# Attention read-out and gated FFN on one core: a new order for the loads of x, for the output of batch 0 and for the last rows

## The chip, the core and the metric

The kernel runs on one core of a Trainium2 chip. The metric is the device time in microseconds (us), the median of repeated runs; a lower time is better. A profile of one execution gives a trace, and every time "in the trace" below counts from the start of that execution's span, which is 228.7 us long.

## The reference, cut to what matters

There are two stages. The first is a cross attention between `x` (8 batches, 8 heads, 512 tokens, 64 channels) and `state` (the same with 32 slots):

```python
scores = scale * np.matmul(x, state.transpose(0, 1, 3, 2))
...                                  # softmax over the 32 slots
xread = np.matmul(a, state)          # 512 rows of each head
scores2 = scale * np.matmul(state, x.transpose(0, 1, 3, 2))
...                                  # softmax over the 512 tokens
sread = np.matmul(a2, x)             # 32 rows of each head
return np.concatenate([xread, sread], axis=2)
```

The second is a gated feed-forward block over the 8 x 544 rows, with the heads put side by side (512 channels, 1536 hidden):

```python
gate = 1.0 / (1.0 + np.exp(-(x @ w_gate)))
val = x @ w_val
return gate * val @ w_out
```

## The kernel before, in words

All instructions are written out in an order set by hand (`tc.manual_schedule()`); each engine runs its own in that order and waits on semaphores for the others. One batch at a time is in work.

**Loads.** `load_x(b, ...)` fetches the 1 MB of batch `b` into one of three `stg` buffers `xf`, with a DMA (L78) issued by the engine that is handed in. `cast_x` (L99) turns it to bf16 (`xb`, two buffers). The weight columns 0 to 255 of gate and value come by the SyncE queue in float32 (`wf`, L356) and are cast on an engine (L90). All other weights come by the GpSimd queue with the cast in the DMA: `load_w` (L83) and `load_wo` (L93). `gate()` (L87) is a one-column GpSimd copy that reads x of batch 1: what is behind it in the GpSimd queue starts when that has landed.

**Attention of batch b.** The transposed `xT` is made on TensorE for batches 0 and 1 (L114, L119), and from batch 2 on by four DMA transposes in the SyncE queue (`at_xT_dma`, L124). `S_mm` (L130) makes the scores in two halves, `S_exp` (L135) their exponentials on ScalarE, `n_sum` (L148, L150) and `n_mul` (L171) the normalised `ab` on VectorE. `aT_dma` (L192) transposes that by DMA; `at_Eb` (L141) is a cast on GpSimd. `n_tok`, `n_split` (L156 to L165), `sr_mm` (L208, L211), `sr_inv` and `sr_fin` (L216, L224) are the softmax over the tokens, whose result for all batches is kept in `XS`.

**FFN of batch b.** `xread` is never formed: the weights are multiplied with the state instead (`sw_mm`, L234), copied to `SW` (L272), and `gv_mm` (L286) multiplies `SW` with `aT`. `gv_th` (L296) is the tanh on ScalarE, `gv_glu` (L301) the product on VectorE. `out_mm` (L314) multiplies the result `glu` with `wo`: twelve calls a batch, call `k` doing four of the twelve hidden blocks of a chunk of 128 tokens; before, calls 0 to 2 make chunk 0, 3 to 5 chunk 1, and so on. The finished chunk is copied on ScalarE (L318) and stored through the SyncE queue (L320).

**Order.** A long hand-written prologue does the loads and the attention of batches 0 and 1 and their `gv_mm`. Then comes the loop over `b` from 1 to 8 with twelve steps `f`: step `f` of round `b` makes `gv_mm(b, f)`, `out_mm(b - 1, f)` and a part of the attention of batch `nb = b + 1`. Round 1 has no `gv_mm`. "Batch" 8 is the group of the 256 slot rows (`XS`), stored before in four pieces of 32 rows a chunk (L324). The last chunk of batch 7 is cut in three pieces (`out_last`, L327 to L340).

**Buffers.** The eight PSUM banks are shared out: two `gv`, one `outp` (OU), four `swp`, one `at`. `gv_mm` takes both `gv` banks, one for the gate, one for the value: the value bank is free again when `gv_glu` has read it. In round 1 the two `gv` banks hold the output of batch 0. `res`, the output copy in SBUF, has three buffers.

Of the kernel before, what the change touches and what calls it, by code (L numbers as in the profile page):

```python
# [8 lines left out]
FP = mybir.dt.float32  # L9
# [7 lines left out]
def kernel(  # L17
# [14 lines left out]
    nc = tc.nc  # L32
    B, H, S, D = x.shape
    Ns = state.shape[2]
    SC = S + Ns
# [7 lines left out]
    wp = ctx.enter_context(tc.tile_pool(name="wp", bufs=1))  # L43
# [26 lines left out]
    def load_x(b, eng, parts=1, hold=None):  # L70
        xf = stg.tile((128, H, 4, D), FP, name="xf")
        if hold is not None:

            hold.memset(xf[:, 0, 0, 0:1], 0.0)
        v = x[b].rearrange("h (p c) d -> p h c d", c=4)
        n = H // parts
        for i in range(parts):
            eng.dma_start(xf[:, n * i:n * i + n], v[:, n * i:n * i + n])  # L78
        xfs[b] = xf
# [2 lines left out]
        src = (moe_w_gate, moe_w_val)[w].rearrange("(k p) n -> p k n", p=128)  # L82
        nc.gpsimd.dma_start((wg, wv)[w][:, :, lo:lo + n], src[:, :, lo:lo + n])  # L83

    def gate():

        nc.gpsimd.tensor_copy(pre[:, 1:2], xfs[1][:, 0, 0, 0:1])  # L87

    def cast_w(w, cp):
        cp((wg, wv)[w][:, :, 0:256], wfs[w])  # L90
# [1 line left out]
    def load_wo(q):  # L92
        nc.gpsimd.dma_start(wo[:, 4 * q:4 * q + 4],  # L93
                            moe_w_out.rearrange("(k p) n -> p k n", p=128)[:, 4 * q:4 * q + 4])

    def cast_x(b, cp, lo, n):
        if b not in xbs:
            xbs[b] = xp.tile((128, 4, H, D), BF, name="xb")
        cp(xbs[b].rearrange("p c h d -> p h c d")[:, lo:lo + n], xfs[b][:, lo:lo + n])  # L99
# [21 lines left out]
    def at_xT_dma(b):  # L121
        xT = xT_tile(b)
        for c in range(4):
            nc.sync.dma_start_transpose(xT[:, :, c], xbs[b][:, c].rearrange("p h d -> p (h d)"))  # L124

    def S_mm(b, i, place):
        ps = held["S", b, i] = place[0].tile((128, 4, 2, 2, Ns), FP, name="Sp", tag=place[1])
        for jj in range(2):
            for c in range(4):
                nc.tensor.matmul(ps[:, c, :, jj], xTs[b][:, 2 * i + jj, c], sTz[:, b, 2 * i + jj], start=True, stop=True)  # L130

    def S_exp(b, i):
        if b not in E1s:
            E1s[b] = ap_.tile((128, 4, 2, 4, Ns), FP, name="E1")
        nc.scalar.activation(E1s[b][:, :, :, 2 * i:2 * i + 2].rearrange("p c e j n -> p (c e) j n"),  # L135
                             held["S", b, i].rearrange("p c e j n -> p (c e) j n"), AF.Exp, scale=scale)
# [9 lines left out]
    def n_sum(b, i):  # L146
        rs = ap_.tile((128, 8, 2), FP, name="rs")
        nc.vector.tensor_reduce(rs, halfE(b, i), AX.X, ALU.add)  # L148
        ri = held["ri", b, i] = ap_.tile((128, 8, 2), FP, name="ri")
        nc.vector.reciprocal(ri, rs)  # L150
# [16 lines left out]
    def n_mul(b, i, eng):  # L167
        if b not in abs_:
            abs_[b] = ap_.tile((128, 4, 2, 128), BF, name="ab")
        ri = held["ri", b, i]  # L170
        eng.tensor_tensor(abs_[b].rearrange("p c e (j n) -> p (c e) j n", n=Ns)[:, :, 2 * i:2 * i + 2], halfE(b, i),  # L171
                          ri.unsqueeze(3).to_broadcast((128, 8, 2, Ns)), ALU.mult)
# [125 lines left out]
    def gv_glu(b, f):  # L298
        if b not in glus:
            glus[b] = fp.tile((128, NF, n_of(b)), BF, name="glu", bufs=2, padded_shape=(128, NF, 512))  # L300
        nc.vector.scalar_tensor_tensor(glus[b][:, f], held["th", b, f], 1.0, held["gv", b, f][1], ALU.add, ALU.mult)  # L301
# [5 lines left out]

    def out_mm(b, k):
        c, f0 = k // 3, (k % 3) * 4
        if f0 == 0:  # L310
            place = SWP if b == B else GV if b == 0 else OU
            ops[b, c] = place[0].tile((128, 512), FP, name="outp", tag=place[1])
        for f in range(f0, f0 + 4):
            nc.tensor.matmul(ops[b, c], glus[b][:, f, c * 128:(c + 1) * 128], wo[:, f],  # L314
                             start=(f == 0), stop=(f == NF - 1))
        if f0 == 8:
            res = fp.tile((128, 512), FP, name="res")
            nc.scalar.activation(res, ops[b, c], AF.Copy, scale=0.5)  # L318
            if b < B:
                nc.sync.dma_start(rows_of(b, c), res)  # L320
            else:
                for i in range(4):
                    r0 = (4 * c + i) * SC + S
                    nc.sync.dma_start(out[r0:r0 + Ns], res[i * Ns:(i + 1) * Ns])  # L324

    def out_last(b, c):

        res = fp.tile((128, 512), FP, name="res")
        for lo, n in ((0, 256), (256, 128), (384, 128)):
            cs = slice(lo, lo + n)  # L330
            ps = p_sw.tile((128, 512), FP, name="outp", tag="swp")[:, :n]
            for f in range(NF):
                nc.tensor.matmul(ps, glus[b][:, f, c * 128:(c + 1) * 128], wo[:, f, cs],  # L333
                                 start=(f == 0), stop=(f == NF - 1))
            if lo == 256:
                nc.scalar.activation(res[:, cs], ps, AF.Copy, scale=0.5)
                nc.scalar.dma_start(rows_of(b, c)[:, cs], res[:, cs])
            else:
                nc.vector.tensor_scalar(res[:, cs], ps, 0.5, None, op0=ALU.mult)
                nc.sync.dma_start(rows_of(b, c)[:, cs], res[:, cs])  # L340
# [8 lines left out]
    sf = wp.tile((128, 16, D), FP, name="sf")  # L349
    nc.sync.dma_start(sf, state.rearrange("b h (u l) d -> (b h u) l d", l=16))  # L350
    load_x(0, nc.sync, 2)
    load_x(1, nc.sync)
    wfs = []
    for src in (moe_w_gate, moe_w_val):
        wf = wp.tile((128, 4, 256), FP, name="wf", bufs=2)
        nc.sync.dma_start(wf, src.rearrange("(k p) n -> p k n", p=128)[:, :, 0:256])  # L356
        wfs.append(wf)
    make_identity(nc, ident)
    nc.vector.memset(sTz, 0.0)
    for e in range(2):  # L360
# [24 lines left out]
    def pad(b, n=1):  # L385
        for e in range(2):
            rows = slice(e * 64, (e + 1) * 64)
            nc.gpsimd.tensor_copy(sTz[rows, b:b + n, :, e], sTc[rows, b:b + n])

    cast_x(0, vec, 2, 2)  # L390
    cast_x(0, pool, 4, 2)
    cast_x(0, act, 0, 2)
# [11 lines left out]
    S_mm(0, 0, SWP)  # L404
    S_exp(0, 0)
    warm(12, SWP)
    gate()
    load_w(0, 256, 256)
    S_mm(0, 1, AT)
    cast_x(1, act, 4, 4)  # L410
# [80 lines left out]
    load_wo(0)  # L491
    load_wo(1)
    load_wo(2)
    gv_glu(0, 5)
    sw_cp(1, 512, 1, 1, vec)
    sw_visit(1, 512, 512, 0)
# [2 lines left out]
    sr_mm(1, AT)  # L499
    sw_cp(1, 512, 1, 0, vec)  # L500
    gv_mm(1, 1, GV)
    load_x(3, nc.scalar)
    gv_th(1, 1)
    sw_visit(0, 1024, 512, 0)
    sw_visit(0, 1024, 512, 1)
# [59 lines left out]
    cast_x(3, pool, 0, 4)  # L565
    cast_x(3, pool, 4, 4)
    at_xT_dma(2)
    at_xT_dma(3)

    for b in range(1, B + 1):  # L570
        nb = b + 1 if b + 1 < B else None
        if b == 1:
            for i in range(2):
                S_mm(nb, i, (AT, GV)[i])
                S_exp(nb, i)
                n_sum(nb, i)
                n_mul(nb, i, nc.vector)
            aT_dma(nb)
        for f in range(NF):
            v, q = f // 6, f % 6  # L580
            if nb is not None and q == 0:
                sw_wide(nb, v)
                sw_cp(nb, v, 0, 0, act)
                sw_cp(nb, v, 0, 1, act)
            for first in (nb is not None and q == 0, nb is None or q > 0):
                if first and b > 1:
                    gv_mm(b, f, SWP if b == B and f % 2 else GV)
                    gv_th(b, f)
                    gv_glu(b, f)
                elif not first and (b < B or f < 9):  # L590
                    out_mm(b - 1, f)
            if nb is not None:
                if q == 0:
                    sw_cp(nb, v, 1, 0, vec)
                elif q in (1, 3, 4):
                    k = {1: 3, 3: 4, 4: 5}[q]
                    sw_cp(nb, v, k // 2, k % 2, act)
                if f in (1, 2) and b > 1:
                    S_mm(nb, f - 1, AT)
                    S_exp(nb, f - 1)  # L600
                elif f in (6, 7):
                    n_tok(nb, f - 6)
                    if f == 7:
                        n_split(nb, 0)
                elif f == 8:
                    n_split(nb, 1)
                elif f == 9:
                    sr_mm(nb, AT)
                    sr_inv(nb)
                elif f == 10:  # L610
                    sr_fin(nb)
                if f in (2, 4) and b > 1:
                    n_sum(nb, f // 2 - 1)
                elif f in (3, 5) and b > 1:
                    n_mul(nb, f // 2 - 1, nc.vector)
                if f == 3:
                    at_Eb(nb)
                    if nb + 2 < B:
                        load_x(nb + 2, nc.sync)
                elif f == 5 and b > 1:  # L620
                    aT_dma(nb)
                    if nb + 1 < B:
                        cast_x(nb + 1, pool, 0, 4)
                        cast_x(nb + 1, pool, 4, 4)
                        at_xT_dma(nb + 1)
# [33 lines left out]
```

The softmax here doesn't subtract the row's maximum and nothing guards it: scores larger than these inputs give would overflow.

## Time and profile before

The time is 231.14 us (median of 3 runs, 230.85 to 231.76).

| engine | busy, us | share of the span |
|---|---|---|
| TensorE (PE) | 218.5 | 96% |
| VectorE (DVE) | 141.4 | 62% |
| ScalarE (ACT) | 131.2 | 57% |
| GpSimd (POOL) | 42.5 | 19% |

The kernel moves 28.09 MB by DMA. Times to landing (from the issue to the last byte's semaphore), from the page's list of DMA issues: a load of x through SyncE 6.4 us in the median, the one through ScalarE (batch 3) 14.8, the one through GpSimd (batch 2) 9.4, the three pieces of `wo` 16.1 in the median.

How to read it: in a group line, the name left of the arrow is written and the one right of it is read, `xN` counts instructions, and the time in brackets is how long the engine stood idle before them and who ended that. SPq, ACTq and POOLq are the queues of instructions that issue DMAs. "PE busy" includes the pipeline, so a stop of TensorE is read from a bracket, not from the share.

### The profile page before, as it was taken

To read this page: it belongs to the slowest core of one execution; us is meant where nothing else is said; L and a number is where in the kernel's file an instruction comes from. 1 tells how busy PE (TensorE), PEld (TensorE's weight loads), DVE (VectorE), ACT (ScalarE), POOL (GpSimd) and SP (SyncE) were. 2 spreads that over 40 slices of the span, in tenths; PEclk is the share of its full clock that TensorE was granted. 3 is DMA by queue.
4 is the path that set the end of the run, shared out by engine and by line. 5 is a ranking of instruction groups with operands and counts; after the bars stand their busy time and mean duration, and the time that the engine had idled before them with its cause. 6 is when DMAs were issued, how large, how long until landed. Compare 5 with 4: busy or idle time off the path is not lost.

```text
span 228.7 us, 4759 instructions
## 1 busy us (share of the span) xinstructions
PE 218.5 (96%) x1856; PEld 113.0 (49%) x1856; DVE 141.4 (62%) x234; ACT 131.2 (57%) x246; POOL 42.5 (19%) x75
## 2 busy tenths in 40 slices
PE   7578999989999999999999999999999999999994
PEld 7463345444554444444444544454445444466743
DVE  2499889975368854886388647874687533422301
ACT  3587877655667476746666567556765444423311
POOL 1399921240015000600060006000200000000000
PEclk9889999999999999999999999999999999999999
DMA  6999999942866243724272431253122111121113
GB/s 218 347 177 174 215 281 246 186 74 59 211 224 221 49 92 123 247 46 95 93 231 82 83 118 46 73 88 116 46 72 69 47 46 49 50 80 55 49 33 105
DMA packets 38790, 28.09 MB, mean 123 GB/s; under 512 B 20976, under 2 KB 34160, under 8 KB 38768
## 3 DMA queue, kind: packets, MB, share of 16 engines
q1 hardware_dynamic: 32560, 21.44, 33.8%
q0 software_dynamic: 5024, 5.24, 13.0%
q10 hardware_dynamic: 1184, 1.11, 1.7%
q8 instruction: 14, 0.23, 0.4%
q14 instruction: 8, 0.07, 0.1%
HBM read 18.35 MB, written 8.91 MB: 119 GB/s over the span
## 4 chain that ended last, share of the span: by engine, by line
PE 78%; DMA 10%; POOL 6%; SPq 3%; issue 1%; ACT 0%; DVE 0%; POOLq 0%; ACTq 0%
PE outp L314 37%; PE gvp L286 28%; DMA xf<-in_x_dram 8%; PE gvp L289 5%; PE swp L234 4%; SPq L124 3%; DMA xT<-xb 2%; POOL Eb L141 1%; PE srp L211 1%; PE outp L333 1%; PE Sp L130 1%; POOL wg L83 1%; POOL ab L171 1%; POOL xb L99 1%; POOL wv L90 1%
## 5 line engine op out<-in xcount | busy, mean ns | idle before, releaser
L301 DVE SCALAR_TENSOR_TENSOR glu<-th,gvp 128x512 bf16<-128x512 f32 (+1 forms) x108 | 70.3, 657 | 63.9 <-ACT th L296 48.6
L314 PE MATMUL outp<-wo,glu 128*128 128x512 bf16 x396 | 97.8, 379 | 0.0
L296 ACT ACTIVATE th<-gvp 128x512 f32<-128x512 f32 (+1 forms) x108 | 61.6, 575 | 62.1 <-PE gvp L286 50.7
L286 PE MATMUL gvp<-aT,SW 128*128 128x512 bf16 x384 | 96.3, 380 | 0.1
L286 PEld LDWEIGHTS <-SW 128*128 128x128 bf16 x384 | 36.2, 98 | 45.1 <-issue 4.2
L314 PEld LDWEIGHTS <-glu 128*128 128x128 bf16 x396 | 37.5, 98 | 41.0 <-issue 0.4
L272 ACT CAST SW<-swp 128x512 bf16<-128x512 f32 (+1 forms) x78 | 42.2, 579 | 2.9 <-PE swp L234 1.6
L318 ACT ACTIVATE res<-outp 128x512 f32<-128x512 f32 x33 | 19.7, 597 | 19.7 <-PE outp L314 17.5
L141 POOL CAST Eb<-E 128x256 bf16<-128x256 f32 x32 | 12.4, 429 | 98.7 <-ACT E L135 98.7
L99 POOL CAST xb<-xf 128x1024 bf16<-128x1024 f32 (+1 forms) x13 | 14.6, 1147 | 20.6 <-DMA xf<-in_x_dram 20.6
L272 DVE CAST SW<-swp 128x512 bf16<-128x512 f32 x20 | 13.4, 683 | 2.7 <-PE swp L234 2.7
L171 DVE TENSOR_TENSOR ab<-E,ri 128x512 bf16<-128x512 f32 x14 | 13.7, 980 | 0.1
L156 DVE TENSOR_REDUCE E<-E 128x128 f32<-128x512 f32 x12 | 12.3, 1033 | 0.0
L234 PE MATMUL swp<-wg,sTc 64*32 64x256 bf16 (+1 forms) x256 | 11.9, 328 | 0.2 <-ACT E L135 0.2
L148 DVE TENSOR_REDUCE rs<-E 128x16 f32<-128x512 f32 x16 | 10.8, 678 | 0.9 <-ACT E L135 0.9
L234 PEld LDWEIGHTS <-sTc 64*32 64x32 bf16 x512 | 6.2, 91 | 10.4 <-issue 7.7
L135 ACT ACTIVATE E<-Sp 128x512 f32<-128x512 f32 x16 | 9.6, 608 | 1.8 <-PE Sp L130 1.8
L234 PE MATMUL swp<-wv,sTc 64*32 64x256 bf16 (+1 forms) x256 | 10.4, 324 | 0.2 <-POOL wv L90 0.2
L130 PE MATMUL Sp<-sTz,xT 128*128 128x64 bf16 x128 | 7.0, 199 | 1.7 <-ACT xT L119 0.7
L130 PEld LDWEIGHTS <-xT 128*128 128x128 bf16 x128 | 6.1, 102 | 4.9 <-ACT xT L119 0.8
L216 DVE RECIPROCAL r<-srp 128x128 f32<-128x128 f32 x8 | 7.6, 951 | 1.1 <-PE srp L211 1.1
L347 PE MATMUL warm<-ident 128*128 128x128 bf16 x56 | 6.1, 300 | 1.4 <-POOL ident masks.py:199 1.4
(53 smaller groups left out, 104.0 us busy)
## 6 DMA issues: line engine op xcount, KB each, us to landing
out_dram<-res SPq DMA_DIRECT2D x31, 256.0 KB, 2.4
xf<-in_x_dram SPq DMA_DIRECT2D x5, 1024.0 KB, 6.4
wo<-in_moe_w_out_dram POOLq DMA_DIRECT2D x3, 512.0 KB, 16.1
xf<-in_x_dram SPq DMA_DIRECT2D x2, 512.0 KB, 5.6
wg<-in_moe_w_gate_dram POOLq DMA_DIRECT2D x2, 512.0 KB, 7.1
wv<-in_moe_w_val_dram POOLq DMA_DIRECT2D x2, 512.0 KB, 7.8
xf<-in_x_dram POOLq DMA_DIRECT2D x1, 1024.0 KB, 9.4
xf<-in_x_dram ACTq DMA_DIRECT2D x1, 1024.0 KB, 14.8
```

The lines of the kernel that those rows point to most:

```text
L99: cp(xbs[b].rearrange("p c h d -> p h c d")[:, lo:lo + n], xfs[b][:, lo:lo + n])
L130: nc.tensor.matmul(ps[:, c, :, jj], xTs[b][:, 2 * i + jj, c], sTz[:, b, 2 * i + jj], start=True, stop=True)
L141: nc.gpsimd.tensor_copy(Ebs[b][:, c], E1s[b][:, c])
L156: nc.vector.tensor_reduce(held["E4", b][:, e].rearrange("p j n -> p (j n)"), E1s[b][:, :, e].rearrange("p c j n -> p (j n) c"), AX.X, ALU.add)
L171: eng.tensor_tensor(abs_[b].rearrange("p c e (j n) -> p (c e) j n", n=Ns)[:, :, 2 * i:2 * i + 2], halfE(b, i), ri.unsqueeze(3).to_broadcas ...
L234: nc.tensor.matmul(pss[e][j * Ns:(j + 1) * Ns, o:o + n], sTc[rows, b, j], (wg, wv)[w][rows, j, lo:lo + n], start=True, stop=True)
L272: cp(*sw_left.pop((b, lo, w, e)))
L286: nc.tensor.matmul(ps, SWs[b][:, g, w, fs], aTs[b][:, :, g], start=(g == 0), stop=(g == 1))
L296: nc.scalar.activation(th, held["gv", b, f][0], AF.Tanh, scale=0.5)
L301: nc.vector.scalar_tensor_tensor(glus[b][:, f], held["th", b, f], 1.0, held["gv", b, f][1], ALU.add, ALU.mult)
L314: nc.tensor.matmul(ops[b, c], glus[b][:, f, c * 128:(c + 1) * 128], wo[:, f], start=(f == 0), stop=(f == NF - 1))
L318: nc.scalar.activation(res, ops[b, c], AF.Copy, scale=0.5)
```

## The change

1. **x of batch 1** is issued only after VectorE has written one column of its buffer, and that write stands behind the cast of the state in VectorE's order. The two `wf` loads move behind it. The gate on it stays.
2. **x of batch 3** is loaded through the GpSimd queue, right behind the three pieces of `wo`, in place of the ScalarE queue.
3. **Output of batch 0**: two chunks of tokens in turn, so that hidden blocks 8 to 11, which read the third piece of `wo`, are wanted later.
4. **xT of batch 3** is transposed in step 5 of round 1, behind `aT` of batch 2 and two stores, and no longer ahead of them.
5. **Round 2** makes the scores of batch 3 one step later: `S_mm` in steps 2 and 3 in place of 1 and 2, and `n_sum`, `n_mul`, `at_Eb`, `aT_dma` and the cast of batch 4 a step later with them. x of batch 4 is loaded in step 6 of round 1 in place of 3.
6. **`res`** has four buffers in place of three.
7. **The slot rows** are stored in one DMA a chunk in place of four.

Its purpose is that the loads which are needed first have the DMA engines to themselves, and that the SyncE queue issues less at the end.

```diff
-    def gate():
+    def gate(landed):
-        nc.gpsimd.tensor_copy(pre[:, 1:2], xfs[1][:, 0, 0, 0:1])
+        nc.gpsimd.tensor_copy(pre[:, 1:2], landed)
+    def load_wf(w):
+        wfs[w] = wp.tile((128, 4, 256), FP, name="wf", bufs=2)
+        nc.sync.dma_start(wfs[w], (moe_w_gate, moe_w_val)[w].rearrange("(k p) n -> p k n", p=128)[:, :, 0:256])
...
     def out_mm(b, k):
         c, f0 = k // 3, (k % 3) * 4
+        if b == 0:
+            c, f0 = k // 6 * 2 + k % 2, k % 6 // 2 * 4
...
-            res = fp.tile((128, 512), FP, name="res")
+            res = fp.tile((128, 512), FP, name="res", bufs=4)
...
-                for i in range(4):
-                    r0 = (4 * c + i) * SC + S
-                    nc.sync.dma_start(out[r0:r0 + Ns], res[i * Ns:(i + 1) * Ns])
+                nc.sync.dma_start(out.rearrange("(b s) d -> b s d", s=SC)[4 * c:4 * c + 4, S:SC], res)
...
     load_x(0, nc.sync, 2)
-    load_x(1, nc.sync)
-    wfs = []
-    for src in (moe_w_gate, moe_w_val):
-        wf = wp.tile((128, 4, 256), FP, name="wf", bufs=2)
-        nc.sync.dma_start(wf, src.rearrange("(k p) n -> p k n", p=128)[:, :, 0:256])
-        wfs.append(wf)
+    wfs = {}
...
+    load_x(1, nc.sync, 1, nc.vector)
+    load_wf(0)
+    load_wf(1)
     cast_x(0, vec, 2, 2)
...
-    gate()
+    gate(xfs[1][:, 0, 0, 0:1])
...
     load_wo(2)
+    load_x(3, nc.gpsimd)
...
-    load_x(3, nc.scalar)
...
     at_xT_dma(2)
-    at_xT_dma(3)
...
-                if f in (1, 2) and b > 1:
-                    S_mm(nb, f - 1, AT)
-                    S_exp(nb, f - 1)
+                g = f - (b == 2)
+                if g in (1, 2) and b > 1:
+                    S_mm(nb, g - 1, AT)
+                    S_exp(nb, g - 1)
...
-                if f in (2, 4) and b > 1:
-                    n_sum(nb, f // 2 - 1)
-                elif f in (3, 5) and b > 1:
-                    n_mul(nb, f // 2 - 1, nc.vector)
-                if f == 3:
+                if g in (2, 4) and b > 1:
+                    n_sum(nb, g // 2 - 1)
+                elif g in (3, 5) and b > 1:
+                    n_mul(nb, g // 2 - 1, nc.vector)
+                if b == 1 and f == 5:
+                    at_xT_dma(nb + 1)
+                if g == 3:
                     at_Eb(nb)
-                    if nb + 2 < B:
-                        load_x(nb + 2, nc.sync)
-                elif f == 5 and b > 1:
+                if nb + 2 < B and f == (6 if b == 1 else 3):
+                    load_x(nb + 2, nc.sync)
+                if g == 5 and b > 1:
                     aT_dma(nb)
```

More of the change, by code (lines that the diff above doesn't have):

```diff
@@ L321, in out_mm @@
             else:
-                for i in range(4):
-                    r0 = (4 * c + i) * SC + S
-                    nc.sync.dma_start(out[r0:r0 + Ns], res[i * Ns:(i + 1) * Ns])
+                nc.sync.dma_start(out.rearrange("(b s) d -> b s d", s=SC)[4 * c:4 * c + 4, S:SC], res)
     def out_last(b, c):
-        res = fp.tile((128, 512), FP, name="res")
+        res = fp.tile((128, 512), FP, name="res", bufs=4)
         for lo, n in ((0, 256), (256, 128), (384, 128)):
```

## The prediction

> **What bounds the kernel now.** I began with the page's chain of work that ended last.
>
> ```profile
> PE 78%; DMA 10%; POOL 6%; SPq 3%; issue 1%; ACT 0%; DVE 0%; POOLq 0%; ACTq 0%
> ```
>
> TensorE carries 78% of the chain. The busy times of the stretch from the first output matmul to the last chunk say why: 174.56 us long, TensorE busy all of it.
>
> ```profile
> 48.34:222.90 174.56, 174.56 (x1341) 86.15 (x1335) 103.74 (x173) 97.64 (x186) 18.49 (x32) 1.00 0.34 96
> ```
>
> The matmul count is unchanged. So only three places can pay: the start before TensorE runs full (20.98 us), the stop between 45.58 and 48.34, and the tail after 222.9.
>
> The start, VectorE's timeline:
>
> ```profile
> 11.23 0.69 DVE L99 CAST xb<-xf 128x1024 bf16<-128x1024 f32 x1 [0.56 <-DMA xf<-in_x_dram]
> ...
> 18.52 1.87 DVE L171 TENSOR_TENSOR ab<-E,ri 128x512 bf16<-128x512 f32 x1
> ```
>
> From 11.23 to 20.39 VectorE never rests, and its last product releases TensorE's transposes at 20.54. So x of batch 1, landed at 11.21, sets the start; batch 0 does not.
>
> The stop in the middle, TensorE's timeline and the chain of waits in order of time (start, us, what):
>
> ```profile
> 46.02 0.20 PE L130 MATMUL Sp<-sTz,xT 128*128 128x64 bf16 x1 [0.21 <-DMA xT<-xb]
> 46.51 0.55 PE L130 MATMUL Sp<-sTz,xT 128*128 128x64 bf16 x13 [0.28 <-DMA xT<-xb]
> 46.99 0.39 PE L234 MATMUL swp<-wg,sTc 64*32 64x512 bf16 x1
> 47.57 0.41 PE L234 MATMUL swp<-wg,sTc 64*32 64x512 bf16 x7 [0.20 <-ACT E L135]
> ```
>
> ```profile
> 33.09 2.03 POOL xb L99 x2
> ...
> 37.79 3.24 SPq L124
> 41.03 0.04 issue
> 41.08 5.38 DMA xT<-xb
> ```
>
> xT of batch 2 lands late: its four transposes, issued from 35.13, land at 46.46. The gaps between matmul starts, less each matmul's columns at the full clock, leave 0.38, 0.46 and 0.37 us: 1.2 us lost. The DMA view of 39 to 42 us shows what is in the way:
>
> ```profile
> q0 software_dynamic: 329, 0.33, 65.3%
> q10 hardware_dynamic: 321, 0.32, 32.8%
> q1 hardware_dynamic: 272, 0.07, 17.6%
> ```
>
> wo (q0), x of batch 3 (q10) and the transposes (q1) share the engines, which are full.
>
> **What the Trainium skill says.** "DMA: Bandwidth & Descriptors", "Queues, rings and completion order": each DMA engine goes round-robin between queues by packet, and a semaphore increment lands only after that engine's earlier writes, on all queues. The lines above agree with the first (near equal counts); the second fits wo's last landing at 44.92 just before the first transpose's, 45.14. Section "Issuing engines are not separate DMA queues": another issuer gives no more bandwidth. So edit 2 only reorders. "GPSIMD Engine Reference", "1. Specifications": GpSimd shares the SBUF interface with VectorE instructions of two SBUF inputs. The trace agrees: `n_mul` takes 0.71 us in the median and 1.87 beside GpSimd casts.
>
> **The change, part by part.**
>
> *Hold on x of batch 1.* VectorE's cast of the state ends at 4.82; a one-column memset ends about 4.9 (GpSimd's of one column take 0.1 us). SyncE then issues at about 5.0 in place of 2.20. First packets follow an issue by 1.05 us (state) to 1.17 (transposes at 46.35): 6.1 us. The queue ahead, state and batch 0, drains at about 6.7: the 1024th 1 KB packet ends at 6.69. So the engines do not run dry, with 0.6 us to spare, and because the queue is served in order, batch 1 lands when it did. What may change is a laggard: 15 of the 16 engines had batch 0's second half by 7.34, one at 8.25; that one has batch 1 at 11.21, the others by 10.75. If the shorter queue cures it, VectorE starts up to 0.46 earlier; n_sum also waits for the exponentials, which would then move too. I can't see the laggard's cause: gain 0 to 0.5, I take 0.2. If the 0.6 is misjudged: up to 0.6 lost.
>
> *x of batch 3 behind wo.* ScalarE saves one issue (0.43), off the path. GpSimd spends about 0.9 more at 26.6 (batch 2's issue: 0.90), ahead of the pads of `sTz`, then idles until 33.09: nothing. On the DMA engines batch 3 was 1024 packets of 1 KB at 46 to 59 ns: 64 an engine, 2.9 to 3.8 us. Through GpSimd, batch 2 went as 256 packets of 4 KB at 159 to 192 ns: 16 an engine, 2.5 to 3.1. Transposes are the smallest packets, round-robin, and issued last, so they end when the whole pile ends; its size falls by about 0.5 us (0 to 1.3). Transposes then land at 46.0 instead of 46.46. The floor: 16 score matmuls straight after 45.58, the first exponential at 46.2 to 46.8, `sw_mm` at 46.75 in place of 47.57, so at most 0.8 is to be had. I take 0.4. wo lands earlier for want of a rival; it was not waited for.
>
> *Two chunks in turn for batch 0.* Same matmuls. The second `gv` bank is wanted in step 1, at 49.2, and its exponential is read by 48.0. Chunk 2 needs chunk 0's bank at 54.4; ScalarE copies it by about 53.4. Round 2 needs chunk 3's bank at 61.6; copied by 61.3. Nothing, hidden behind the matmuls.
>
> *xT of batch 3 later.* The SyncE queue becomes: aT of batch 2 (50.4, four at 1.28), two stores (0.5 each), four transposes from 56.7, landed about 63.5; wanted, a step later, at 66.4. The load of batch 4 is behind them (62.2), landed about 67.5; GpSimd casts it after `Eb`, by 72.8. Hidden.
>
> *Round 2 a step later.* Here I expect a loss. `n_mul` of batch 3's second half leaves step 5 (73.07) for step 6, behind the token sum, which ends at 76.42. Step 7's `gv_glu` was at
>
> ```profile
> 76.74 0.69 DVE L301 SCALAR_TENSOR_TENSOR glu<-th,gvp 128x512 bf16<-128x512 f32 x1 [0.33 <-ACT th L296]
> 77.34 1.04 DVE L156 TENSOR_REDUCE E<-E 128x128 f32<-128x512 f32 x1
> 78.42 0.29 DVE L163 CAST Es<-E 128x256 bf16<-128x256 f32 x1
> 78.63 0.68 DVE L301 SCALAR_TENSOR_TENSOR glu<-th,gvp 128x512 bf16<-128x512 f32 x1
> ```
>
> and moves to 76.94. The row at 78.63 moves by the same 0.2; it ended at 79.31, and the value matmul of step 9 started at 79.36. TensorE therefore loses about 0.2 once (0.1 to 0.4), queued behind nothing but that bank. aT of batch 3 is issued at 77.1 in place of 73.82, lands at 83.3, wanted at 84.8. xT of batch 4 comes behind it: last landing 86.06 + 2.6 = 88.6, wanted at 88.3 to 88.4 plus the 0.2. Between 0 and 0.6 lost; I take 0.1.
>
> *res and rows.* A fourth buffer frees the copy that waited for a landing until 60.92: off the path. At the tail, the page's timeline has
>
> ```profile
> 223.88 1.36 SPq L324 DMA_DIRECT2D out_dram<-res  x3
> 225.34 0.88 SPq L340 DMA_DIRECT2D out_dram<-res  x2
> ```
>
> The last-but-one store could go at 224.65 (its data is done at 224.63), but the very last waits for VectorE at 225.84 and was issued at 225.87 already. So no issue time is won on the path; only the landings thin out: the last took 1.71 us, the last row store of the first chunk 1.72, the very first 1.63. Gain 0.1 to 0.3; I take 0.15.
>
> Sum: -0.2 - 0.4 + 0.2 + 0.1 - 0.15 = -0.45, so 230.7.
>
> **Rivals.**
>
> A (48%): the sum, 230.7.
>
> B (30%), everything pays: the laggard is cured (0.5, and 0.15 more because the first product runs beside less GpSimd work), the stop shrinks to its floor (0.8), the tail gives 0.25, VectorE absorbs the step: 231.14 - 1.7 = 229.4. For it: the stop is there and the DMA is full. Against: it needs the transposes landed by about 45.6, 0.4 us earlier than I find.
>
> C (12%), slower, a new wait takes the old one's place: batch 1 finds empty queues (+0.6), GpSimd's DMA packets lag on some engines (of the second wo piece, thirteen engines landed by 38.47, the last at 41.25) and now carry batch 3 ahead of the transposes (+0.4), VectorE costs 0.4, xT of batch 4 is late by 0.5, tail -0.1: 231.14 + 1.8 = 232.9. For it: the thin margins of 0.6 and 0.2. Against: they hold on paper.
>
> D (10%): gains and losses cancel, the transfers were hidden: 231.2.
>
> **How the numbers follow.** The likeliest is A. Range: B's 229.4 less 0.2 to 232.0, between D and C, so that about one in ten is left out at each end. Within 0.5% means 229.98 to 232.30: A and D; A's own spread hands 1 point to faster. Faster 0.31, same 0.57, slower 0.12.
>
> **What would show it.** In the profile after: x of batch 1 issued near 5.0 and the cast at 11.2 or up to 0.5 earlier; score matmuls of batch 2 with their last bracket on xT smaller; no wait of TensorE in round 1; `n_mul` at about 76 with step 9's value matmul pushed by 0.2; the score matmuls of batch 4 at 88 with no DMA bracket; the last store still issued right behind VectorE. Wrong if VectorE's cast of batch 1 starts after 11.5, if the transposes land after 46.5, or if TensorE's work between 48 and 222 gains a stop of over 0.5.

## The result and the profile after

The kernel after takes 237.97 us in the median (236.97 to 238.83, 4 runs), the kernel before, run beside it, 231.07 (230.85 to 231.76, 4 runs). The ratio is 1.029, with a 95% interval of 1.024 to 1.035: the change made the kernel slower. The predicted 230.7 and its range of 229.2 to 232.0 both miss, on the wrong side.

The profiled execution after has a span of 235.5 us, against 228.7 before. All times of "the trace" below count from the start of such an execution. I read it in the order of the prediction, first the chain of work that ended last, by engine:

```profile
PE 76%; DMA 12%; POOL 5%; SPq 2%; issue 1%; DVE 0%; ACT 0%; POOLq 0%; ACTq 0%
```

DMA went from 10% to 12%. Then the busy times from the first output matmul to the last chunk:

```profile
51.17:226.05 174.88, 174.88 (x1341) 86.32 (x1335) 103.64 (x173) 97.55 (x186) 18.54 (x32) 1.00 0.35 96
```

The same 1341 matmuls take 174.88 us, 174.56 before. So 0.3 of the 6.8 us by which the span grew lie in this stretch, and the rest lies at the three places that the prediction had looked for gains in.

**The start.** The chain in order of time (start, us, what), and VectorE's timeline:

```profile
5.00 0.04 DVE xf L74
5.03 0.02 issue
5.05 7.57 DMA xf<-in_x_dram
...
12.74 0.72 POOL pre L87
```

```profile
12.71 0.69 DVE L103 CAST xb<-xf 128x1024 bf16<-128x1024 f32 x1 [2.83 <-DMA xf<-in_x_dram]
...
18.84 0.69 DVE L192 COPY aT<-aTp 128x1024 bf16<-128x1024 bf16 x1 [0.38 <-PE aTp L182]
...
20.45 1.99 DVE L175 TENSOR_TENSOR ab<-E,ri 128x512 bf16<-128x512 f32 x1
```

The load was issued at 5.05, as predicted, but it landed at 12.62, not at 11.2. VectorE begins its cast 1.48 us later than before. Another 0.56 is added until the last product: VectorE now waits 0.38 for TensorE's transposes at 18.84. From 13 to 17 us TensorE's granted clock was 0.50 of the full one, against 0.97 before. TensorE's transposes of `ab` start at 22.58 in place of 20.54: 2.04 us late. Before, and then after:

```profile
20.54 0.61 PE L178 MATMUL aTp<-ident,ab 128*128 128x128 bf16 x8 [1.03 <-DVE ab L171]
```

```profile
22.58 0.61 PE L182 MATMUL aTp<-ident,ab 128*128 128x128 bf16 x8 [1.27 <-DVE ab L175]
```

The DMA view of 6 to 9 us shows where the load lost time. Its first line is the busy share of the 16 DMA engines in 40 equal slices, in tenths; a packet counts whole in the slice in which it starts. Before, and then after:

```profile
DMA  9999999999999999989999999999999999996897
```

```profile
DMA  9999999996775993013822678899999999999979
```

The row of nines has a hole from 6.7 to 7.9, in which the engines start few packets. From 7 to 8 us, 340 packets of the loads started before, and 144 after.

**The stop in the middle.** TensorE's timeline:

```profile
48.34 0.20 PE L134 MATMUL Sp<-sTz,xT 128*128 128x64 bf16 x1 [0.20 <-DMA xT<-xb]
48.87 0.20 PE L134 MATMUL Sp<-sTz,xT 128*128 128x64 bf16 x1 [0.32 <-DMA xT<-xb]
49.34 0.55 PE L134 MATMUL Sp<-sTz,xT 128*128 128x64 bf16 x13 [0.27 <-DMA xT<-xb]
```

There are now three brackets on `xT` instead of two. The transposes of batch 2 were issued from 37.55 and landed at 49.29: 11.74 us, against 11.33 before. TensorE goes from the end of its last prologue `gv_mm` to the first output matmul in 3.55 us in place of 2.76. This is the "stop in the middle" of the runs below.

**The tail.** The timeline of SyncE's queue, and the list of DMA issues from 223 us on (the last number of a line is the time from issue to landing):

```profile
224.12 3.13 SPq L329 DMA_DIRECT2D out_dram<-res  x2
227.85 2.39 SPq L345 DMA_DIRECT2D out_dram<-res  x2
```

```profile
out_dram<-res SPq DMA_DIRECT2D x1, 128.0 KB, 6.3
out_dram<-res ACTq DMA_DIRECT2D x1, 64.0 KB, 5.9
out_dram<-res SPq DMA_DIRECT2D x1, 64.0 KB, 5.4
```

The same list before, from 221 us on:

```profile
out_dram<-res SPq DMA_DIRECT2D x9, 64.0 KB, 1.7
out_dram<-res SPq DMA_DIRECT2D x1, 128.0 KB, 2.1
out_dram<-res ACTq DMA_DIRECT2D x1, 64.0 KB, 1.7
```

The three pieces of the last chunk need 5.4 to 6.3 us to land, where they took 1.7 to 2.1. From the end of the last matmul to the end of the kernel, the tail, it is 7.04 us, 3.39 before. The semaphores, which a DMA raises by 16 in all, show what is ahead of them. The row store issued at 224.12 has twelve of its sixteen increments at once, at 225.21, and the last four between 229.53 and 230.33. The store issued at 226.71 has twelve at 227.67, and four from 232.47 to 233.72. Every piece of the last chunk has twelve engines through early (by 230.85, 231.55 and 233.01) and four late, the last at 234.11, 234.29 and 234.48. So four of the sixteen engines carry all of the 256 KB of a row store, and the pieces behind them queue on those four, the one that ScalarE issued through its own queue (5.9 us) like the others.

The sum of the parts: 2.0 + 0.8 + 0.3 + 3.65 = 6.75 us, from one trace of each kernel.

### The profile page after: what moved, and what is told of

It reads as the page before. It is cut to its first block, busy times and chain, and to the rows that moved or that the text cites. A ratio compares the mean times of both kernels' runs of the same rounds, so it can differ in the third digit from the quotient of the medians.

```text
span 235.5 us, 4753 instructions
## 1 busy us (share of the span) xinstructions
PE 221.0 (94%) x1856; PEld 114.5 (49%) x1856; DVE 141.4 (60%) x235; ACT 131.2 (56%) x246; POOL 43.0 (18%) x76
## 4 chain that ended last, share of the span: by engine, by line
PE 76%; DMA 12%; POOL 5%; SPq 2%; issue 1%; DVE 0%; ACT 0%; POOLq 0%; ACTq 0%
PE outp L321 36%; PE gvp L290 27%; DMA xf<-in_x_dram 8%; PE gvp L293 4%; PE swp L238 4%; DMA xT<-xb 3%; SPq L128 2%; DMA sf<-in_state_dram 2%; PE srp L215 1%; PE Sp L134 1%; PE outp L338 1%; POOL Eb L145 1%; POOL wg L83 1%; POOL ab L175 1%; POOL xb L103 1%
## 5 line engine op out<-in xcount | busy, mean ns | idle before, releaser
L325 ACT ACTIVATE res<-outp 128x512 f32<-128x512 f32 x33 | 19.7, 598 | 19.9 <-PE outp L321 19.6
L152 DVE TENSOR_REDUCE rs<-E 128x16 f32<-128x512 f32 x16 | 10.8, 678 | 1.7 <-ACT E L139 1.7
L238 PEld LDWEIGHTS <-sTc 64*32 64x32 bf16 x512 | 6.3, 91 | 10.2 <-issue 7.5
L238 PE MATMUL swp<-wv,sTc 64*32 64x256 bf16 (+1 forms) x256 | 10.7, 332 | 0.0
L134 PE MATMUL Sp<-sTz,xT 128*128 128x64 bf16 x128 | 7.7, 205 | 1.8 <-DMA xT<-xb 0.8
L134 PEld LDWEIGHTS <-xT 128*128 128x128 bf16 x128 | 6.6, 106 | 5.4 <-DMA xT<-xb 1.8
```

Of the source, the lines that this page charges most:

```text
L238: nc.tensor.matmul(pss[e][j * Ns:(j + 1) * Ns, o:o + n], sTc[rows, b, j], (wg, wv)[w][rows, j, lo:lo + n], start=True, stop=True)
```

## The experiments

My theory after the two traces: (1) the hold lets the DMA queue run dry; (2) x of batch 3 at the end of the GpSimd queue makes the transposes slower and not faster; (3) the single row store runs on four engines. The rival to (1) is that a late x only moves work which TensorE's own lateness hides. The rival to (2) is that the transposes are late only because x of batch 1 was. The rival to (3) is that the tail is long for the lateness of everything else. Every ratio is to runs of the kernel before on the same chip, with its 95% interval in brackets. Several chips were used, and what is read from a single trace varies: in the seven traces of kernels that load x of batch 3 through ScalarE, the kernel before among them, the transposes of batch 2 take 10.95 to 11.44 us from their first issue to their last landing, and the stop in the middle is 2.44 to 3.67 us. The 0.8 of the kernel after at that stop (3.55 against 2.76) lies within this.

### Each edit taken out of the kernel after

**Rows in four stores again.**

```diff
-                nc.sync.dma_start(out.rearrange("(b s) d -> b s d", s=SC)[4 * c:4 * c + 4, S:SC], res)
+                for i in range(4):
+                    r0 = (4 * c + i) * SC + S
+                    nc.sync.dma_start(out[r0:r0 + Ns], res[i * Ns:(i + 1) * Ns])
```

> The changed kernel with the slot rows stored in four DMAs a chunk again, nothing else undone. Theory (the single store per chunk runs on few DMA engines, so the end waits for it): the time from the last matmul to the end goes from 7.0 us back to 3.4, the kernel from 238.0 to about 234.4. Rival (the tail is long because the kernel arrives in a different state there, or because the stores of the last chunk are slow by themselves): the row stores still land 6 to 7 us after their issue and the time stays above 237.

Measured: 233.34 us, ratio 1.005 (1.002 to 1.008). The tail is 3.45 us, as before the change. x of batch 1 is late as in the kernel after, it lands at 13.44. The transposes take 11.63 us, but TensorE comes so late that none of its brackets is on `xT`; the stop is 2.19 us.

**No hold on x of batch 1.**

```diff
-    load_x(1, nc.sync, 1, nc.vector)
+    load_x(1, nc.sync)
```

> The changed kernel with x of batch 1 loaded without waiting for VectorE, nothing else undone. Theory (the hold lets the DMA queue run dry): x of batch 1 lands at about 11.2 in place of 12.6, TensorE runs full from about 21.0 in place of 23.0, and the kernel gains 2.0: about 236.0. Rival (the late landing is a matter of some slow DMA engines, whatever the issue time): it lands after 12, and the time stays at 237 to 238.

Measured: 235.82 us, ratio 1.016 (1.008 to 1.023). x lands at 10.70 and TensorE's transposes of `ab` start at 20.02. The stop in the middle is still there and longer, 3.91 us: the transposes take 11.76 us from their issue although x of batch 1 was in time. That speaks against the rival to (2). The tail is 7.81 although nothing at the start was late, which speaks against the rival to (3).

**x of batch 3 on ScalarE again.**

```diff
     load_wo(2)
-    load_x(3, nc.gpsimd)
...
     gv_mm(1, 1, GV)
+    load_x(3, nc.scalar)
```

> The changed kernel with x of batch 3 loaded through the ScalarE queue at its old place, nothing else undone. Theory (behind wo in the GpSimd queue its 4 KB packets meet the transposes and slow them): the transposes of batch 2 land 11.3 us after the cast of x of batch 2 in place of 11.8 to 12, TensorE's stop before the output of batch 0 goes from 2.0 to 1.2 us, and the kernel gains 0.5 to 0.8: about 237.3. Rival (the stop grew because everything was late by then): no change within 0.3.

Measured: 236.39 us, ratio 1.018 (1.010 to 1.025). The transposes take 11.25 us, as before, and the stop is 2.44. The interval of this ratio just meets that of the kernel after (1.024 to 1.035).

**All three taken out**, by the three diffs above. This leaves two chunks in turn, xT of batch 3 later, round 2 a step later and the fourth `res`.

> The changed kernel with three of its edits undone: the rows in four stores, no hold, x of batch 3 through ScalarE at its old place. What is left is the output of batch 0 in pairs of chunks, the later transposes of batch 3, round 2 a step later, and the fourth res buffer. Theory (the three edits are the whole loss but 0.2): within 0.4 us of before, at most 0.3 slower. Rival (the rest costs something of its own): 1 us or more slower.

Measured: 231.45 us beside 231.48, ratio 1.001 (0.997 to 1.004). The three edits are the whole loss; the others together cost and gain nothing beyond 0.4%.

### Each edit alone, put into the kernel before

**The single row store alone.**

```diff
-                for i in range(4):
-                    r0 = (4 * c + i) * SC + S
-                    nc.sync.dma_start(out[r0:r0 + Ns], res[i * Ns:(i + 1) * Ns])
+                nc.sync.dma_start(out.rearrange("(b s) d -> b s d", s=SC)[4 * c:4 * c + 4, S:SC], res)
```

> The kernel before with the slot rows stored in one DMA a chunk, nothing else changed. Theory (few engines): each row store lands 6 to 7 us after its issue in place of 1.6 to 1.8, and the stores of the last chunk behind it land late on the same engines; 231.1 + 3.6 = 234.7. Rival (the tail needs the other edits): within 0.5 us of 231.1.

Measured: 235.77 us, ratio 1.012 (1.005 to 1.020). The tail of its trace is 7.88 us, the two row stores land 6.2 and 7.9 us after their issue. In this trace TensorE also stops in round 2, a thing of its own that I come back to:

```profile
62.73 0.59 PE L286 MATMUL gvp<-aT,SW 128*128 128x512 bf16 x2 [1.02 <-ACT res L318]
```

**Row stores of two blocks, two a chunk.** If the count of engines follows the outermost dimension of the store, this must be worse than one store of four blocks, though it is more DMAs of less data each.

```diff
-                for i in range(4):
-                    r0 = (4 * c + i) * SC + S
-                    nc.sync.dma_start(out[r0:r0 + Ns], res[i * Ns:(i + 1) * Ns])
+                for i in range(2):
+                    nc.sync.dma_start(out.rearrange("(b s) d -> b s d", s=SC)[4 * c + 2 * i:4 * c + 2 * i + 2, S:SC],
+                                      res[2 * i * Ns:(2 * i + 2) * Ns])
```

> The kernel before with the slot rows of a chunk stored in two DMAs of two blocks of 32 rows. Theory (a store runs on as many DMA engines as its outermost dimension has blocks, and always on the same first ones): two engines carry everything, each store of half the bytes lands as late as or later than the single store did, the end is 9 to 12 us after the last matmul in place of 7 to 7.8 with one store, and the time is 236 to 240. Rival (a store over several blocks is slow by its length or shape, not by its engines): half the bytes land in half the time, and the time is between 231.5 and 234.

Measured: 240.02 us, ratio 1.035 (1.027 to 1.044), and a tail of 12.45 us. The list of DMA issues from 220 us on:

```profile
out_dram<-res SPq DMA_DIRECT2D x5, 128.0 KB, 10.8
...
out_dram<-res SPq DMA_DIRECT2D x1, 64.0 KB, 10.4
```

Now fourteen increments come at once and two late: the store issued at 221.22 has fourteen at 222.28 and the last two at 226.57 and 226.62. The next three land at 230.17, 233.59 and 236.15, 3.2 us apart in the mean. Each gives 64 KB to each of its two engines. In the kernel after, each of the four engines also gets 64 KB of a store, and its two stores land 3.4 us apart. In the kernel before the 16 engines get 4 KB each, and a store is landed after 1.6 to 1.8 us. So the size follows from the 64 KB that each engine has to write, 3.2 to 3.4 us from one landing to the next.

**The hold alone.**

```diff
     load_x(0, nc.sync, 2)
-    load_x(1, nc.sync)
-    wfs = []
-    for src in (moe_w_gate, moe_w_val):
...
+    load_x(1, nc.sync, 1, nc.vector)
+    wfs = []
+    for src in (moe_w_gate, moe_w_val):
...
     cast_x(0, vec, 2, 2)
```

> The kernel before with only the hold on x of batch 1 (issue behind VectorE's cast of the state, the two wf loads behind it). Theory (the DMA queue runs dry before the held load's first packets come): x of batch 1 lands at 12.4 to 13.4 in place of 10.7 to 11.2, TensorE's clock stays halved longer, the matmuls run full 2 us later, and the time is 231.5 + 2.0 = 233.5, less what the stop before the output of batch 0 gives back because TensorE comes later to it. Rival (the hold hurts only with the other edits): within 0.5 us of before.

Measured: 233.35 us, ratio 1.006 (1.003 to 1.009). x is issued at 5.20 and lands at 12.99, TensorE's transposes of `ab` start at 23.17. Part of that is another wait: VectorE stands 1.32 us for the first `wf` load, which this edit also moves behind the hold. The time is clearly longer, so what is behind does not hide the lateness, as the rival to (1) would have it.

**The hold, released earlier.** It waits for a GpSimd memset of a tile of its own instead of VectorE's cast. The load is still held, but issued so early that the engines should not run out of packets. The identity and the other first memsets move ahead of it.

```diff
     load_x(0, nc.sync, 2)
-    load_x(1, nc.sync)
+    make_identity(nc, ident)
...
+    late = wp.tile((128, 2048), FP, name="late")
+    nc.gpsimd.memset(late, 0.0)
+    load_x(1, nc.sync, 1, nc.gpsimd)
     wfs = []
...
-    make_identity(nc, ident)
...
```

> The kernel before with the hold on x of batch 1, but released by GpSimd after a filler memset of 128x2048 (about 1.8 us), so that SyncE issues it at 3.5 to 3.8 us instead of 5.0 to 5.5 or 2.2. Theory (a held load costs only when the queue runs dry before its first packets): it lands at 10.6 to 11.3 as without a hold, no dip of the DMA rate at 7 us, and the time is within 0.4 us of before. Rival (holding it, or having the wf loads right behind it, is what makes some DMA engines late): it lands after 12.2 as with the late hold, and the time is 1 to 2 us longer.

Measured: 231.96 us beside 232.27, ratio 0.999 (0.997 to 1.002). The load is issued at 3.46 and lands at 11.20, as without a hold. The same view of 6 to 9 us as above:

```profile
DMA  9998999899989999899998989999999999999999
```

No hole, no loss: it is not the hold as such that costs, nor the `wf` loads behind it. In the four kernels with the late hold 142 to 219 packets of 1 KB start between 7 and 8 us, in all twelve others 291 to 375. (In this one trace TensorE's transposes of `ab` start at 21.16 all the same, since VectorE's product before them took 2.51 us in place of 1.87.)

**x of batch 3 behind the output weights alone.**

```diff
     load_wo(2)
+    load_x(3, nc.gpsimd)
...
     gv_mm(1, 1, GV)
-    load_x(3, nc.scalar)
```

> The kernel before with only x of batch 3 moved behind wo in the GpSimd queue. Theory (4 KB packets among the transposes): the last transpose of batch 2 lands 11.6 to 11.8 us after the first is issued in place of 11.2 to 11.3, and the kernel loses 0.3 to 0.5: about 231.9. Rival, the prediction's step (fewer and larger packets shorten the pile): it lands after 10.8 or less and the kernel gains 0.4.

Measured: 233.24 us, ratio 1.007 (1.004 to 1.010). The transposes take 12.75 us and the stop is 5.04, 2.3 more than before. The direction was expected, the size is several times what I had expected (11.6 to 11.8 us, and 0.3 to 0.5 us of loss). TensorE comes to the stop as early as in the kernel before, its last `gv` matmul starting at 45.37 in both traces, and waits all of it out.

### What in the place of x of batch 3 costs

**Ahead of all three pieces of the output weights**, and **ahead of the third only**, each in the kernel before and through the GpSimd queue. The queue is as long as in the last run; only what stands at its end differs. The diff is that of the first; in the second the line stands between `load_wo(1)` and `load_wo(2)`.

```diff
+    load_x(3, nc.gpsimd)
     load_wo(0)
     load_wo(1)
     load_wo(2)
...
     gv_mm(1, 1, GV)
-    load_x(3, nc.scalar)
```

> The kernel before, with x of batch 3 loaded through the GpSimd queue, but ahead of all three pieces of the output weights and not behind them. Theory 1 (the transposes are slow as long as x's 4 KB packets share the engines with them; 185 ns for 256 B, against 18): x of batch 3 is through by about 38, what is left beside the transposes are the 1 KB packets of the weights, and the four transposes take no longer than in the kernel before (11.3 us from the first issue, and not the 12.7 of the load behind the weights); ratio to before 0.998 to 1.003. Theory 2 (the length of the GpSimd queue alone counts: all its bytes are ahead of the transposes wherever x stands in it): the transposes take 12.3 us or more and the ratio is 1.005 or more.

> As the last one, but ahead of the third piece of the output weights only. Theory 1: x of batch 3 ends by about 42, the last 2 to 3 us of the transposes stand beside 1 KB packets of the weights: 11.3 to 12.2 us, ratio 1.000 to 1.005. Theory 2: 12.3 us or more, ratio 1.005 or more.

Measured: 230.89 us, ratio 0.997 (0.995 to 0.999), and 230.74, ratio 0.994 (0.992 to 0.997), beside 231.84. The transposes take 10.71 and 10.87 us, no more than in the seven traces named above, against 12.75 with x at the end of the same queue. So the length of the queue is not what costs; what stands at its end is. Both kernels are faster than expected, and the second not by this stop, which is 3.03 us in its trace (2.13 in the first); what it gains from stays open. The DMA view of 45 to 47 us, first of the kernel with x behind the weights alone, then with x ahead of all of them (in a queue's line: packets, MB, time of its packets as a share of the 16 engines; above 100% when packets of an engine overlap):

```profile
DMA  9009400900490099009530900790099009400003
...
q1 hardware_dynamic: 238, 0.06, 121.5%
q0 software_dynamic: 13, 0.05, 6.1%
```

```profile
DMA  9999999999999999999820000003597999999999
...
q1 hardware_dynamic: 1564, 0.38, 94.9%
```

With the last thirteen packets, nearly all of 4 KB, still in q0 the packets of the transposes (q1) start in bursts, 238 in 2 us. Without them it is 1564. In the first of the two, a 256-byte packet of a transpose takes 187 ns in the median (191 in the kernel after), in the second 18. Why a transpose's packet takes ten times as long beside so few others, these runs don't tell. Nor do they tell the size of the packets from other properties of this load, such as that it has no cast.

**Behind the transposes of batch 2**, in SyncE's queue, in the kernel after with rows in four stores and no hold.

```diff
-    load_x(3, nc.gpsimd)
...
+    at_xT_dma(2)
+    load_x(3, nc.sync)
     cast_x(3, pool, 0, 4)
     cast_x(3, pool, 4, 4)
-    at_xT_dma(2)
```

> The changed kernel with the rows in four stores, no hold, and x of batch 3 loaded in the SyncE queue right behind the four transposes of batch 2, so that it is out of their way. Theory (x of batch 3 beside the transposes is what makes TensorE stop): the transposes land 9 to 10.5 us after the first issue, the stretch from the last gv matmul to the first output matmul goes from 2.8 to 1.9 us, and the time is 0.6 to 0.9 below before: about 230.8. Rival (wo alone fills the engines as long): stop unchanged, time within 0.3 of before.

Measured: 229.88 us beside 232.27, ratio 0.991 (0.987 to 0.994): faster than both kernels. It differs from the run with all three edits taken out (ratio 1.001) only in the place of x of batch 3. The transposes take 8.97 us and land at 44.82, before TensorE wants them. In TensorE's timeline no bracket on `xT` is left there:

```profile
45.16 0.63 PE L134 MATMUL Sp<-sTz,xT 128*128 128x64 bf16 x16
45.72 0.39 PE L238 MATMUL swp<-wg,sTc 64*32 64x512 bf16 x1
46.30 0.41 PE L238 MATMUL swp<-wg,sTc 64*32 64x512 bf16 x7 [0.20 <-ACT E L139]
```

What is left of the stop, 1.91 us, is the scores, their exponential and `sw_mm`. The stop explains 0.85 of the 2.4 us between the medians; where the rest comes from, these runs don't show.

**The same with x of batch 1 in two halves**, and the GpSimd queue's gate on the second.

```diff
-    load_x(1, nc.sync)
+    load_x(1, nc.sync, 2)
-    gate(xfs[1][:, 0, 0, 0:1])
+    gate(xfs[1][:, 4, 0, 0:1])
```

> e10_x3_late with x of batch 1 loaded in two halves (heads 0 to 3 first), the gate on the second. Theory (the landing of x of batch 1 sets VectorE's chain): VectorE's cast of the first half starts at about 10.0 in place of 11.0, its chain ends 0.4 to 0.6 earlier, as then the first exponential holds it, and the time is 0.3 to 0.5 below e10_x3_late. Rival (the gate and the GpSimd queue behind it set the start): no difference.

Measured: 229.92 us, ratio 0.989 (0.986 to 0.993): no different. In the trace, VectorE's cast of batch 1 starts at 10.78, against 10.72 without the halves. The first half had landed by 9.53; until 10.78 VectorE waited for `xT` of batch 0 and copied its part of it. So neither the landing nor the gate set the start there, but batch 0 did.

**The same without the later step of round 2.**

```diff
-                g = f - (b == 2)
+                g = f
```

> e10_x3_late without the later step in round 2: scores of batch 3 in steps 1 and 2 again. Theory (the later step makes VectorE push back one value matmul by 0.16 us): that stop goes, but the transposes of batch 3, now behind aT of batch 2 and two stores, land at about 63.3, when the scores are wanted at about 63.8: between 0.2 faster and 0.3 slower than e10_x3_late. Rival (the step is needed): TensorE stops over 0.5 us at those scores.

Measured: 230.26 us, ratio 0.990 (0.987 to 0.994): no different in the median. The trace shows that the step then takes the place of a wait, for `xT` of batch 3 that now comes late (0.69 us, as the rival expected, though the time does not show it):

```profile
64.77 0.32 PE L134 MATMUL Sp<-sTz,xT 128*128 128x64 bf16 x5 [0.69 <-DMA xT<-xb]
```

With the step there is no such bracket; in its place TensorE loses 0.16 once on the value bank and waits 0.34 for `xT` of batch 4 at 87.76.

## Why the prediction was wrong, step by step

**Hold on x of batch 1: -0.2 predicted, +2.0 measured.** The step that failed is "So the engines do not run dry, with 0.6 us to spare". It took the first packet to come 1.05 to 1.17 us after its issue, from DMAs issued into other conditions, and took the load to run at full rate from there. Batch 0 has 1024 packets of 1 KB, and the 1025th starts at 6.68, so the first packet of batch 1 came at the latest 1.63 us after its issue. But twelve packets that start between 6.65 and 7.5 take 260 to 830 ns, where 46 is the median, and the full rate is back only at about 7.9. The prediction gave this at most 0.6 us of loss. The hole itself is worth less: the middle engine lands x of batch 1 at 10.6 in place of 10.2. But one to four engines end much later, and all sixteen must be through. In the four kernels with this hold the last engine lands at 12.62 to 13.44, in the traces of the other kernels at 11.24 or before. The prediction had hoped that the hold would cure a laggard, and it made worse ones. Why these engines lag stays open. Nor was there much to win: the prediction says that batch 0 does not set the start, but its work held VectorE until 10.67 in the kernel before, and until 10.78 in the run with halves. And the 0.56 that VectorE then loses, 0.38 of it waiting for TensorE, was in no step.

**x of batch 3 behind wo: -0.4 predicted, +0.8 in the pair of traces, and +2.3 on the stop with a ratio of 1.007 as a single edit.** The step that failed is "they end when the whole pile ends; its size falls by about 0.5 us". I summed the DMA time of the packets, as if any mix of them would flow at one rate. What counted here is what the transposes still have beside them in their last microseconds: 11.6 to 12.75 us with x at the end of the queue, in four traces, and 10.7 to 10.9 with the same bytes ahead of the weights. The large packets that looked cheap per byte were the bad neighbours there. That the transposes were the DMA to look at, and that x of batch 3 stood in their way, was right: with x out of the way the whole stop above its floor goes, 2.76 to 1.91 us, which is 0.85 and close to the "at most 0.8" of the prediction.

**Two chunks in turn, xT of batch 3 later: nothing predicted.** Right, as far as 0.4% can tell: with the three bad edits taken out, the rest gives 1.001 (0.997 to 1.004).

**Round 2 a step later: +0.2 predicted, 0.16 measured, and by the mechanism named.** VectorE's timeline after:

```profile
80.36 1.04 DVE L160 TENSOR_REDUCE E<-E 128x128 f32<-128x512 f32 x1
81.43 0.29 DVE L167 CAST Es<-E 128x256 bf16<-128x256 f32 x1
81.64 0.68 DVE L305 SCALAR_TENSOR_TENSOR glu<-th,gvp 128x512 bf16<-128x512 f32 x1
```

The `glu` product behind the token sum frees the value bank, and the matmul start after 82.00 comes 0.16 us later than its columns at the full clock account for. Late `xT` of batch 4 was put at 0.1, with 0 to 0.6 as bounds: 0.09 in the trace.

One reading of the prediction is too broad. `n_mul` took 1.76 and 1.87 us beside GpSimd's work at the start, but later 1.09 to 1.16 beside its casts of x, and 0.73 beside its casts for `Eb`. Only 0.15 of rival B rested on it.

**res: "off the path".** Right for the traces of before and after. But with three buffers the copy's wait for a landing is close to the path: it stopped TensorE by 1.02 us in the trace of the single row store, shown above, and by 0.72 in that of the hold alone. No trace of a kernel with four buffers has this bracket.

**Rows: -0.15 predicted, +3.65 measured.** The step that failed is "only the landings thin out". I priced a DMA by its issue and took the landing from stores of the same bytes, without asking on how many engines it would run. The Trainium skill states the rule, in "DMA: Bandwidth & Descriptors", "Why a DMA increments its semaphore by 16 and not by 1": the number of engines is the largest one up to 16 that divides the slowest dimension of both sides; a DMA on fewer engines uses the lowest-numbered ones; and the issuing sequencer posts the increments of the others at once. The new store's slowest dimension on the side of the output is 4. The traces agree on the numbers: 12 increments at once with 4 blocks, 14 with 2, none with 32 rows. They do not name the engines, but each DMA behind a row store has as many late engines as the row store had. The prediction drew on other sections of that page, for the queues, and not on this one, for the shape. No rival had it either: C, the one that ended slower, named the start (+0.6) and the transposes (+0.4), but counted -0.1 for the tail.

Two of the losses overlap: the hold alone gives 1.006 and x of batch 3 alone 1.007, but both together, with the rows in four stores, no more than 1.005. The hold makes TensorE late at the stop in the middle, and a late TensorE waits less for late transposes: the stop is 5.04 us with x of batch 3 moved alone, and 3.55 and 2.19 in the two traces with both. For the rows, 1.012 (1.005 to 1.020) alone against a step from 1.005 to 1.029 in company, the few runs leave the size open, around the 3.65 us of the tail.

Two of the three signs of being wrong that the prediction named came true, VectorE's cast after 11.5 (12.71) and the transposes after 46.5 (49.29); the third, a stop of over 0.5 us between 48 and 222, did not. The chance of 12% for slower was too small for a change with margins of 0.6 and 0.2 us, each taken from DMAs in other conditions.

## What to carry to other kernels

Before DMAs are merged, look at the outermost dimension of both sides: a merged store may run on four engines in place of sixteen, and every store behind it, from another queue too, waits on those four. A load that is held back should be issued early enough to leave no hole in the row of DMA nines; here 3.3 us ahead of its turn cost nothing, and 1.4 us ahead cost 0.6% of the kernel. When a transfer that is waited for shares the engines with bulk loads, what stands beside it at its end can count more than the sum of the bytes: here it paid to put the bulk that is wanted last behind it, not in front.

## What was not expected of the hardware

- A 64 KB share of a store took one DMA engine 3.2 to 3.4 us, counted from one landing to the next, with two engines in use as with four.
- While the last dozen 4 KB packets were left in the GpSimd queue, between 45 and 47 us, 256-byte packets of DMA transposes took 187 to 191 ns in the median. They took 18 ns in the same stretch when no load was left. From 42 to 45 us, with more of the 4 KB packets beside them, they took 18 ns too but were fewer: 634 with x behind the weights alone, 1100 in the kernel before.
- After the hole in the queue one to four of the sixteen engines landed up to 2.6 us behind the middle one (12.62 to 13.44 against 10.4 to 10.8).
- TensorE's granted clock stayed at 0.50 from 13 to 17 us after the late start, where it was 0.97 before; around the start of batch 1 it was lowered for 3.4 us in the kernel before (9.8 to 13.2), and for 10.2 in the kernel after (9.3 to 19.6). The lengths fit what the Trainium skill has in "TensorE: Matmul & The Clock Gate", "Part 1: The HAM clock gate (the "warmup" mystery)": half the clock after an idle window of about 3.4 us, until one such window was busy. The two lengths are one and three such windows. But "idle" is not to be taken as without work: in the 3.4 us ahead of the lower clock TensorE was busy for 1.24 us before and 1.58 after.
